# Output tiles whose two row halves swap PSUM banks midway, in a fused attention and feed-forward kernel

## The chip, the cores and the metric

The kernel runs on one core of a Trainium2 chip. The metric is the device time of one launch in microseconds (us), the median over several runs; for the kernel before it is 373.13 us (three runs, 372.79 to 373.79). A profiled execution of the same kernel gives the trace that is read below. The engines are called PE (TensorE matmul), PEld (TensorE weight load), DVE (VectorE), ACT (ScalarE), POOL (GpSimd) and SP (SyncE, which issues the stores).

## The reference

Attention with a softmax whose denominator has one term more, then a feed-forward layer with a squared ReLU. Cut to what matters:

```python
# q, k, v: (8, 12, 448, 64); w_in: (768, 2048); w_out: (2048, 768)
scores = scale * q @ k.T
e = exp(scores - max)
attn = e / (sum(e) + exp(-max) + 1e-9)
x = (attn @ v) laid out as (3584, 768)     # 8 * 448 tokens
r = maximum(x @ w_in, 0)
out = (r * r) @ w_out                      # (3584, 768), float32
```

Inputs come as float32 and are used as float16 on PE; sums are float32.

## The kernel before

**Work.** Batches are b = 0 to 7. Three heads' quads per batch (four heads each) go through scores, exponential, sums and values; the result, transposed, is x for the feed-forward layer. The hidden layer g = (max(x w_in, 0))^2 stands in a ring of two batches (`gs`), and the output is made from it in tiles of 128 tokens, each as two half tiles of 384 columns (`HALF`). A half tile is a sum over 16 blocks f of 128 hidden units.

**How a half tile is summed.** `out_piece` with `rows=True` (L553) cuts the 128 x 128 array in four parts of 64 x 64. For each f it issues four matmuls: two column parts (64 tokens each), and for each the array's upper rows (hidden units 0 to 63 of the block) into one PSUM bank (`op`), the lower rows (64 to 127) into another (`lo`). At the end each bank holds half of the sum, for all 128 tokens. `out_first` (L570) reads bank `op`, scales it and writes the SBUF tile `ot`, on DVE (L576) or on ACT (L574); `out_second` (L578) then reads `lo` on DVE (L580), adds `ot` and stores the half tile through the SP queue (`store`, L539). The order within a half tile is thus: 64 matmuls, first copy, add, store.

**The order is written by hand.** Strings of steps give the order of every instruction on all engines; each engine works its own steps strictly in that order, and semaphores are placed where a step needs another engine's result. The letters that matter here:

- `s` scores of a chunk on PE into one of two double banks (`sp`), `e` its exponential on ACT (L255), which frees the double bank; `v` the chunk's product with the values on PE (seven chunks, 0 to 6, per quad).
- `a` with step 0 to 3: the sum over the chunks on DVE (L439, L441, L443, L445); `S` the column sums on PE (needs `a` step 3, and takes a double bank), `Z` and `M` their logarithm and reciprocal on ACT (L461, L464), `X` the scaled values on DVE (L485).
- `o n,f0,f1`: `out_piece` of half tile n for blocks f0 to f1; `O n,act`: `out_first`, on ACT where act is 1; `Q n`: `out_second`.
- `J` and the letters A to I and U: the hidden layer, on full 128 x 128 matmuls (L663), with ACT and DVE work behind each.

**PSUM.** Eight banks: two double banks for `sp`, and a ring of four single banks (`mp`) which output tiles (two at a time), values (two at a time, `v` 0 until `X`) and the hidden layer share. A new tile takes the bank that was set free first in the written order, and its first matmul waits until the last reader of that bank is done.

**Three stretches hold the steps that the change touches.** The second list of steps (L880) works on batches 1 to 3 and the first 14 half tiles; its part from half tile 6 on ran at about 100 to 131 us. `CYCLE` (L935) is worked twice, for periods 4 and 6, with 14 half tiles each; in each the hidden layer comes first, then scores, exponentials, values and output tiles side by side (about 163 to 217 us and 249 to 304 us). What follows to the end of the kernel is not touched.

Of the kernel before, what the change touches and what calls it, by code (L numbers as in the profile page):

```python
# [17 lines left out]
def kernel(  # L18
# [235 lines left out]
    def exp(out_, in_):  # L254
        nc.scalar.activation(out=out_, in_=in_, func=AF.Exp, scale=scale)  # L255
# [174 lines left out]
    def quad_exp(m, c):  # L430
        exp(chunk_quad(m, c).rearrange("p (o x) -> p o x", o=2), sps.pop(("quad", m, c))[:, :, 0:S])

    def add_quad(m, step):

        a, z = eqs[m, 0], eqs.get((m, 1))
        w = 4 * S
        if step == 0:
            esq[m] = es_pool.tile([128, w], FP16, name="half")
            nc.vector.tensor_add(esq[m], a[:, 0:w], a[:, w:2 * w])  # L439
        elif step == 1:  # L440
            nc.vector.tensor_add(esq[m], esq[m], z[:, 0:w])  # L441
        elif step == 2:
            nc.vector.tensor_add(esq[m][:, 0:2 * S], esq[m][:, 0:2 * S], esq[m][:, 2 * S:w])  # L443
        else:
            nc.vector.tensor_add(esq[m][:, 0:2 * S], esq[m][:, 0:2 * S], z[:, w:w + 2 * S])  # L445
# [17 lines left out]
    def quad_reciprocal(m):  # L463
        nc.scalar.activation(out=zqs[m], in_=zqs[m], func=AF.Exp, scale=-1.0)  # L464
# [415 lines left out]
    for step in """  # L880
        S1 s44 v1,0 Z1 v1,1 v1,2 v1,3 v1,4 v1,5 s45 o0,0,2 v1,6 e44 o0,2,4 a2,0 o0,4,6 a2,1 M1 o0,6,8 s46 o0,8,10 X1 o0,10,12 e45 o0,12,14
        a2,2 a2,3 s47 o2,0,2 w0 e46 o2,2,4 e47 s48 o0,14,16 e48 o2,4,6 S2 O0,0 o2,6,8 o2,8,10 s49 o2,10,12 o2,12,14 Q0 Z2 s50 a3,0 v2,0
        o2,14,16 O2,0 Q2 e49 s51 v2,1 v2,2 v2,3 e50 e51 v2,4 w2 s52 v2,5 v2,6 a3,1 o1,0,2 o1,2,4 M2 o1,4,6 s53 o1,6,8 e52 o1,8,10 s54 e53
        o1,10,12 o1,12,14 s55 X2 e54 o1,14,16 o4,0,2 e55 a3,2 O1,0 s56 o4,2,4 o4,4,6 s57 o4,6,8 y1 o4,8,10 Q1 e56 a3,3 o4,10,12 e57 a4,0
        o4,12,14 s58 o4,14,16 v3,0 S3 v3,1 e58 O4,0 v3,2 v3,3 Z3 Q4 v3,4 a4,1 s59 v3,5 d26 d27 o3,0,2 s60 v3,6 a4,2 M3 o3,2,4 o3,4,6 e59
        o3,6,8 o3,8,10 X3 o3,10,12 s61 o3,12,14 e60 o3,14,16 o5,0,2 s62 o5,2,4 y2 w4 o5,4,6 e61 e62 a4,3 s63 o5,6,8 O3,0 y3 Q3 o5,8,10
        o5,10,12 o5,12,14 e63 a5,0 s64 o5,14,16 S4 O5,1 J0,1 A0 Q5 d24 d25 e64 y4 J1,1 J0,2 w1 J0,6 J1,2 C0 A1 J1,6 J0,5 U0 U1 B0 C1 w6 a5,1
        J1,5 J0,7 J1,7 D0 B1 G1 J1,3 J0,3 Z4 D1 J0,4 E0 J1,4 J2,1 F1 E1 J3,1 J3,2 F0 A2 J2,2 w3 H0 w5 C2 G0 J2,6 A3 U2 J3,6 J2,5 C3 J2,7 U3 M4
        J3,5 a5,2 w7 B2 B3 J3,7 D2 G3 D3 I0 G2 J2,3 J3,3 J2,4 F2 E3 J3,4 E2 s65 v4,0 s66 v4,1 F3 v4,2 H1 v4,3 e65 I1 H2 a5,3 H3 v4,4 v4,5 s67
        e66 o6,0,2 o6,2,4 v4,6 X4 I2 S5 e67 I3 o6,4,6 Z5 o6,6,8 s68 o6,8,10 e68 o6,10,12 s69 v5,0 e69 o6,12,14 o6,14,16 s70 O6,0 v5,1 e70 v5,2  # L890
        v5,3 M5 v5,4 v5,5 v5,6 Q6 a6,0 s71 e71 o7,0,2 o7,2,4 s72 X5 o7,4,6 e72 o7,6,8 o7,8,10 s73 o7,10,12 e73 o8,0,2 s74 o8,2,4 e74 o7,12,14
        a6,1 s75 e75 o7,14,16 a6,2 o8,4,6 s76 e76 o8,6,8 o8,8,10 a6,3 O7,0 s77 e77 o8,10,12 o8,12,14 S6 Q7 o8,14,16 v6,0 s78 v6,1 v6,2 v6,3
        v6,4 Z6 s79 O8,0 e78 v6,5 Q8 v6,6 e79 a7,0 o9,0,2 o9,2,4 M6 s80 o9,4,6 e80 o9,6,8 a7,1 s81 o9,8,10 o9,10,12 o9,12,14 o9,14,16 X6 s83
        e81 d28 o10,0,2 a7,2 s82 o10,2,4 o10,4,6 a7,3 e83 o10,6,8 s85 o10,8,10 O9,0 e82 o10,10,12 S7 Q9 o10,12,14 o10,14,16 v7,0 v7,1 e85 v7,2
        Z7 v7,3 s86 M7 O10,0 s84 v7,4 v7,5 Q10 o11,0,2 v7,6 e84 a8,0 o11,2,4 o11,4,6 o11,6,8 d31 o11,8,10 X7 o11,10,12 d29 o11,12,14 a8,1
        o11,14,16 o12,0,2 o12,2,4 o12,4,6 o12,6,8 O11,1 Q11 o12,8,10 e86 o12,10,12 o12,12,14 a8,2 o12,14,16 v8,0 a8,3 S8 v8,1 O12,1 v8,2 v8,3
        v8,4 v8,5 v8,6 Q12 o13,0,2 o13,2,4 d30 o13,4,6 o13,6,8 Z8 M8 o13,8,10 Y1 o13,10,12 o13,12,14 X8 o13,14,16 O13,1 Y2 Q13
    """.split():
        STEPS[step[0]](*(int(y) for y in step[1:].split(",")))

    def period(b):
# [38 lines left out]
        o0,0,2 F7 e0,0 I5 s0,1 e0,1 o0,2,4 H6 o0,4,6 o0,6,8 s0,2 o0,8,10 e0,2 o0,10,12 s0,3 H7 e0,3 I7 o0,12,14 I6 o0,14,16 s0,4 o1,0,2 e0,4  # L940
        o1,2,4 O0,0 Q0 s0,5 d1 o1,4,6 o1,6,8 s0,6 o1,8,10 e0,5 o1,10,12 s1,0 a0,0 o1,12,14 e0,6 o1,14,16 e1,0 a0,1 s1,1 a0,2 O1,0 e1,1 o2,0,2
        o2,2,4 s1,2 o2,4,6 o2,6,8 e1,2 s1,3 o2,8,10 o2,10,12 a0,3 e1,3 S0 Z0 o2,12,14 Q1 o2,14,16 s1,4 e1,4 v0,0 v0,1 v0,2 v0,3 M0 O2,0 v0,4
        Q2 v0,5 s1,5 o3,0,2 e1,5 s1,6 o3,2,4 a1,0 v0,6 o3,4,6 e1,6 o3,6,8 X0 s2,0 a1,1 o3,8,10 o3,10,12 e2,0 s2,1 a1,2 a1,3 o3,12,14 o4,0,2
        s2,2 e2,1 o4,2,4 o3,14,16 s2,3 o4,4,6 e2,2 O3,0 o4,6,8 e2,3 S1 Q3 o4,8,10 Z1 o4,10,12 o4,12,14 a2,0 v1,0 o4,14,16 s2,4 v1,1 M1 d3 v1,2
        O4,0 e2,4 Q4 v1,3 v1,4 s2,5 v1,5 v1,6 X1 o5,0,2 o5,2,4 e2,5 s2,6 o5,4,6 o5,6,8 a2,1 s3,0 a2,2 e2,6 o6,0,2 e3,0 o5,8,10 a2,3 s3,1 e3,1
        o5,10,12 o5,12,14 s3,2 e3,2 o6,2,4 o5,14,16 s3,3 e3,3 O5,0 o6,4,6 o6,6,8 Q5 S2 o6,8,10 o6,10,12 v2,0 a3,0 s3,4 o6,12,14 o6,14,16 Z2
        O6,0 s3,5 v2,1 v2,2 Q6 e3,4 s3,6 v2,3 v2,4 M2 v2,5 v2,6 X2 o7,0,2 o7,2,4 e3,5 e3,6 o7,4,6 s4,0 o7,6,8 o7,8,10 e4,0 s4,1 e4,1 o8,0,2
# [147 lines left out]
```

## Time and profile before

| | |
|---|---|
| median of three runs | 373.13 us (372.79 to 373.79) |
| profiled execution | 372.36 us, of which the span from first to last instruction is 370.3 us |
| granted TensorE clock | 1.00 |
| PE busy | 361.7 us (98% of the span) |
| ACT busy | 282.4 us (76%) |
| DVE busy | 275.7 us (74%) |

A page of the profile lists busy times, then 40 slices of the span, the DMA queues, the chain of work that ended last, groups of instructions by line, and DMA issues. In group rows, "x2688 | 133.2, 323" means 2688 instructions, 133.2 us in which at least one of them ran, and 323 ns as the mean length of one; after the next bar stands the idle time of the engine before them and what ended it. In a timeline row the first number is the start in us from the span's start, the second the length in us of that merged row; on PE, matmuls overlap, so a row reaches past the start of the next. What counts on PE is the distance from start to start. A row of a wait view reads: who waited, for whom, total us, how often, longest.

### The profile page before, as it was taken

The numbers are of one execution on the slowest core, as the hardware profiler recorded it, in microseconds if no ns is written. First come the engines' busy times: TensorE is split into PE (matmuls) and PEld (weight loads), VectorE is DVE, ScalarE is ACT, GpSimd is POOL, SyncE is SP. The second block draws the span as 40 slices with busy tenths as digits, with TensorE's granted clock in tenths as the row PEclk, the third lists the DMA queues.
The fourth block names the chain that finished last, engine by engine and source line by source line (L and its number), as shares of the span: only waits on it lengthen the run. The fifth ranks groups of instructions, "written<-read, shape, count | busy, mean of one in ns | idle before, by whom it ended". The sixth has DMA issues, their size and how long they took to land.

```text
span 370.3 us, 13666 instructions
## 1 busy us (share of the span) xinstructions
PE 361.7 (98%) x6024; PEld 248.8 (67%) x6024; DVE 275.7 (74%) x484; ACT 282.4 (76%) x413; POOL 62.3 (17%) x96
## 2 busy tenths in 40 slices
PE   8789999999999999999999999999999999999996
PEld 4566556669977755567799965557777765555664
DVE  3888898999987875867887874777878777885441
ACT  6899988987899645689999665679999748794221
POOL 8543350400400330400201060400200000000000
PEclk9999999999999999999999999999999999999999
DMA  8999999999777999905229669854212110001232
GB/s 138 203 205 205 204 198 206 226 225 189 154 146 133 190 181 191 134 2 114 62 58 156 154 118 180 162 64 99 61 53 66 47 62 5 2 0 44 86 85 88
DMA packets 75052, 45.31 MB, mean 122 GB/s; under 512 B 47473, under 2 KB 72945, under 8 KB 74993
## 3 DMA queue, kind: packets, MB, share of 16 engines
q0 software_dynamic: 24752, 22.62, 38.7%
q1 hardware_dynamic: 49952, 21.59, 27.0%
q8 instruction: 47, 0.77, 0.9%
q10 hardware_dynamic: 288, 0.23, 0.2%
q14 instruction: 13, 0.10, 0.1%
HBM read 45.69 MB, written 17.93 MB: 172 GB/s over the span
## 4 chain that ended last, share of the span: by engine, by line
PE 90%; ACT 4%; DVE 2%; DMA 2%; issue 1%; POOL 1%; POOLq 0%; DVEq 0%
PE mp L94 42%; PE mp L663 38%; PE sp L94 9%; ACT et L255 3%; DMA nn<-in_k_dram 2%; PE mp L208 1%; ACT rcp L373 1%; DVE qk L218 0%; ACT rcp L366 0%; DVE half L342 0%; DVE half L441 0%; DVE half L443 0%; DVE half L445 0%; DVE half L348 0%; DVE xt L485 0%
## 5 line engine op out<-in xcount | busy, mean ns | idle before, releaser
L255 ACT ACTIVATE et<-sp 128x896 f16<-128x896 f32 (+2 forms) x173 | 145.2, 899 | 7.6 <-PE sp L94 6.9
L94 PE MATMUL mp<-wout,gs 64*64 64x384 f16 (+1 forms) x2736 | 138.8, 322 | 0.2 <-issue 0.2
L94 PEld LDWEIGHTS <-gs 64*64 64x64 f16 (+1 forms) x2736 | 87.4, 107 | 21.7 <-issue 0.8
L663 PEld LDWEIGHTS <-win 128*128 128x128 f16 x480 | 46.4, 98 | 33.6 <-issue 1.2
L94 PE MATMUL sp<-qk 64*64 64x224 f16 (+1 forms) x1056 | 56.2, 273 | 2.3 <-issue 0.7
L663 PE MATMUL mp<-xt,win 128*128 128x448 f16 (+1 forms) x288 | 54.2, 329 | 0.0
L94 PEld LDWEIGHTS <-qk 64*64 64x64 f16 x1056 | 34.4, 114 | 14.5 <-issue 6.2
L189 POOL COPY flatq<-qk 64x384 f16<-64x384 f16 x20 | 15.3, 763 | 159.4 <-DMA qk<-stage_k 142.7
L94 PE MATMUL mp<-et,vn 64*64 64x448 f16 (+1 forms) x616 | 38.8, 345 | 0.0
L663 PE MATMUL mp<-et,win 128*128 128x448 f16 x144 | 32.8, 352 | 0.0
L576 DVE TENSOR_SCALAR ot<-mp 128x384 f32<-128x384 f32 x34 | 18.9, 556 | 18.0 <-PE mp L94 17.9
L663 PE MATMUL mp<-et,nn 128*128 128x448 f16 (+1 forms) x160 | 32.3, 350 | 0.0
L663 PEld LDWEIGHTS <-nn 128*128 128x128 f16 x216 | 21.0, 98 | 14.7
L666 ACT ACTIVATE qk<-mp 128x448 f32<-128x448 f32 (+1 forms) x33 | 16.8, 532 | 16.0 <-PE mp L663 15.9
L580 DVE SCALAR_TENSOR_TENSOR ot<-mp,ot 128x384 f32<-128x384 f32 x42 | 23.4, 556 | 6.7 <-ACT ot L574 4.0
L485 DVE TENSOR_TENSOR xt<-mp,rcp 128x448 f16<-128x448 f32 x42 | 24.2, 618 | 4.3 <-ACT rcp L464 2.2
L94 PEld LDWEIGHTS <-vn 64*64 64x64 f16 x756 | 22.7, 107 | 6.1 <-issue 0.5
L715 ACT ACTIVATE gs<-mp 128x448 f16<-128x448 f32 x28 | 14.2, 543 | 15.0 <-PE mp L663 13.3
L439 DVE TENSOR_TENSOR half<-et 128x1792 f16<-128x1792 f16 x21 | 23.0, 1097 | 1.2 <-ACT et L255 1.2
L660 DVE CUSTOM_DVE_ANT_0 gs<-mp,rcp 128x448 f16<-128x448 f32 x24 | 14.2, 619 | 13.0 <-ACT rcp L666 7.4
L441 DVE TENSOR_TENSOR half<-half,et 128x1792 f16<-128x1792 f16 x21 | 22.8, 1085 | 0.7 <-DVE half L439 0.5
L710 ACT ACTIVATE gs<-gs 128x448 f16<-128x448 f16 (+1 forms) x36 | 22.4, 657 | 1.1 <-DVE gs L660 1.1
(102 smaller groups left out, 450.2 us busy)
## 6 DMA issues: line engine op xcount, KB each, us to landing
out_dram<-ot SPq DMA_DIRECT2D x52, 96.0 KB, 3.5
out_dram<-ot SPq DMA_DIRECT2D x19, 192.0 KB, 2.0
win<-in_moe_w_in_dram POOLq DMA_DIRECT2D x8, 384.0 KB, 12.9
wout<-in_moe_w_out_dram POOLq DMA_DIRECT2D x4, 768.0 KB, 11.8
vn<-in_v_dram POOLq DMA_DIRECT2D x10, 288.0 KB, 5.6
stage_q<-in_q_dram POOLq DMA_DIRECT2D x4, 676.0 KB, 11.6
stage_k<-in_k_dram POOLq DMA_DIRECT2D x4, 676.0 KB, 14.4
nn<-in_q_dram POOLq DMA_DIRECT2D x8, 224.0 KB, 7.9
```

Source lines behind the costliest of these rows:

```text
L94: return nc.tensor.matmul(out_, lhsT, rhs, start=start, stop=stop)
L189: nc.gpsimd.tensor_copy(km[rows_].rearrange("p h (x o) -> p h x o", o=2)[:, :, :, odd], src[:, :, S // 2 - 32:S // 2])
L255: nc.scalar.activation(out=out_, in_=in_, func=AF.Exp, scale=scale)
L439: nc.vector.tensor_add(esq[m], a[:, 0:w], a[:, w:2 * w])
L441: nc.vector.tensor_add(esq[m], esq[m], z[:, 0:w])
L485: nc.vector.tensor_mul(xts[b][:, 2 * g + i, :], xqs[m][i][:, 0:S], zqs[m][:, i, :])
L576: nc.vector.tensor_scalar(out=ot, in0=op[:, 0:w], scalar1=OUT_SCALE, scalar2=None, op0=ALU.mult)
L580: nc.vector.scalar_tensor_tensor(out=ot, in0=lo[:, 0:w], scalar=OUT_SCALE, in1=ot, op0=ALU.mult, op1=ALU.add)
L660: nc.vector._custom_dve(TENSOR_ADD_SAT, out=out_, in0=ps, in1=t, s0=3.0e38, s1=0.0)
L663: nc.tensor.matmul(out_, lhsT=lhsT, rhs=rhs, start=begins and first, stop=last, skip_group_check=not begins)
L666: nc.scalar.activation(out=t[:, 0:w], in_=src[:, 0:w], func=AF.Copy, scale=scale_)
L710: nc.scalar.activation(out=out_, in_=out_, func=AF.Square)
```

## The change

For 16 of the 21 tiles that are summed by halves of the array's rows (tiles 3 to 6 in the second list, tiles 1 to 6 of each pass of `CYCLE`) the two half tiles of a tile are now summed together. A new step `h t,k` (`turn_piece`), k = 0 to 15, issues eight matmuls, as many as the two blocks of an `o` step that it replaces, at the same places of PE's order. In the first eight pieces (turn 0) the upper rows sum into the bank of half tile 0 and the lower rows into that of half tile 1; in the last eight (turn 1) they change places. So at the end each bank holds a complete sum.

Each bank is then read once: `K t` copies half tile 0 on ACT, `L t` half tile 1 on DVE, each followed by its store. The steps `O` and `Q` of these tiles are gone, and with them the add.

Upper and lower rows must not write one bank at the same time, so turn 1 has to begin after the last matmul of turn 0 is done. This is written as two waits: a step that is marked `*t` in the list waits for the last matmul of turn 0 of tile t, beside what it waited for before, and the first matmul of turn 1 waits for that step. The marked steps are, in the second list, `e70*3`, `e78*4`, `M7*5` (ACT) and `a8,3*6` (DVE); in `CYCLE` `e1,4*1`, `M1*2`, `e3,4*3` (ACT), `a4,0*4`, `a5,0*5` and `a5,3*6` (DVE). The other steps stand in the same order.

```diff
+    def turn_piece(tok, k):
+        if k == 0:
+            turns[tok] = (mp_tile(), mp_tile())
+        turn, k = divmod(k, NFFB // 2)
+        g = gs[:, :, tok % RING:tok % RING + 128]
+        for f in (2 * k, 2 * k + 1):
+            for y in (0, 64):
+                for r in range(2):
+                    x, n = 64 * r, r ^ turn
+                    ins = mm(turns[tok][n][y:y + 64, 0:HALF], g[x:x + 64, f, y:y + 64], wout[x:x + 64, f, HALF * n:HALF * n + HALF],
+                             start=(f == 0 and turn == 0), stop=(f == NFFB - 1 and turn == 1))
+                    if turn and f == 0 and (y, r) == (0, 0):
+                        behind(ins, turned[tok])
+        if turn == 0:
+            turned[tok] = ins
+
+    def behind(ins, other):
+        tc.add_manual_dep(ins.ins, other.ins.name, mybir.DependencyInfo(mybir.DependencyClass.Sync, mybir.DependencyReason.DATA),
+                          reason="sums of the other rows in the same bank")
+
+    def run(steps, text, first=0):
+        for step in text.split():
+            step, _, tile_ = step.partition("*")
+            ins = steps[step[0]](*(int(y) for y in step[1:].split(",")))
+            if tile_:
+                tok = 128 * (first + int(tile_))
+                behind(ins, turned[tok])
+                turned[tok] = ins
+
+    def turn_out(tok, n):
+        ot = osb_pool.tile([128, HALF], FP32, name="ot")
+        src = turns[tok][n][:, 0:HALF]
+        if n:
+            nc.vector.tensor_scalar(out=ot, in0=src, scalar1=OUT_SCALE, scalar2=None, op0=ALU.mult)
+        else:
+            nc.scalar.activation(out=ot, in_=src, func=AF.Copy, scale=OUT_SCALE)
+        store(tok, ot, HALF * n, HALF * n + HALF)
...
 # second list, from half tile 6 on
-        e66 o6,0,2 o6,2,4 v4,6 X4 I2 S5 e67 I3 o6,4,6 Z5 o6,6,8 s68 o6,8,10 e68 o6,10,12 s69 v5,0 e69 o6,12,14 o6,14,16 s70 O6,0 v5,1 e70 v5,2
+        s65 v4,0 s66 v4,1 F3 v4,2 H1 v4,3 e65 I1 H2 a5,3 H3 v4,4 v4,5 s67 e66 h3,0 h3,1 v4,6 X4 I2 S5 e67 I3 h3,2 Z5 h3,3 s68 h3,4 e68 h3,5 s69 v5,0
+        e69 h3,6 h3,7 s70 v5,1 e70*3 v5,2 v5,3 M5 v5,4 v5,5 v5,6 a6,0 s71 e71 h3,8 h3,9 s72 X5 h3,10 e72 h3,11 h3,12 s73 h3,13 e73 h4,0 s74 h4,1 e74
+        h3,14 a6,1 s75 e75 h3,15 a6,2 h4,2 s76 e76 h4,3 h4,4 a6,3 K3 s77 e77 h4,5 h4,6 S6 L3 h4,7 v6,0 s78 v6,1 v6,2 v6,3 v6,4 Z6 s79 e78*4 v6,5
+        v6,6 e79 a7,0 h4,8 h4,9 M6 s80 h4,10 e80 h4,11 a7,1 s81 h4,12 h4,13 h4,14 h4,15 X6 s83 e81 d28 h5,0 a7,2 s82 h5,1 h5,2 a7,3 e83 h5,3 s85
+        h5,4 K4 e82 h5,5 S7 L4 h5,6 h5,7 v7,0 v7,1 e85 v7,2 Z7 v7,3 s86 M7*5 s84 v7,4 v7,5 h5,8 v7,6 e84 a8,0 h5,9 h5,10 h5,11 d31 h5,12 X7 h5,13
...
-        a8,2 o12,14,16 v8,0 a8,3 S8 v8,1 O12,1 v8,2
+        a8,2 h6,7 v8,0 a8,3*6 S8 v8,1 v8,2
...
 # CYCLE
-        s2,2 e2,1 o4,2,4 o3,14,16 s2,3 o4,4,6 e2,2 O3,0 o4,6,8 e2,3 S1 Q3 o4,8,10 Z1 o4,10,12 o4,12,14 a2,0 v1,0 o4,14,16 s2,4 v1,1 M1
+        s2,2 e2,1 h2,1 h1,15 s2,3 h2,2 e2,2 K1 h2,3 e2,3 S1 L1 h2,4 Z1 h2,5 h2,6 a2,0 v1,0 h2,7 s2,4 v1,1 M1*2
...
-        s3,3 e3,3 O5,0 o6,4,6 o6,6,8 Q5 S2 o6,8,10 o6,10,12 v2,0 a3,0 s3,4 o6,12,14 o6,14,16 Z2 O6,0 s3,5 v2,1 v2,2 Q6 e3,4 s3,6
+        s3,3 e3,3 K2 h3,2 h3,3 L2 S2 h3,4 h3,5 v2,0 a3,0 s3,4 h3,6 h3,7 Z2 s3,5 v2,1 v2,2 e3,4*3 s3,6
...
-        a5,3 S5 O12,1 Q12 v5,1
+        a5,3*6 S5 v5,1
...
-    for b in range(FIRST_PERIOD, B, 2):
-        STEPS = period(b)
-        for step in CYCLE.split():
-            STEPS[step[0]](*(int(y) for y in step[1:].split(",")))
+    for b in range(FIRST_PERIOD, B, 2):
+        run(period(b), CYCLE, EARLY // 2 + KC * (b - FIRST_PERIOD) // 2)
```

The functions `exp`, `quad_exp`, `add_quad` and `quad_reciprocal` now return their instruction, so that the marked steps can be made to wait. The lists above are cut and their lines joined; the steps between are the same but for `o`, `O` and `Q` becoming `h`, `K` and `L`.

More of the change, by code (lines that the diff above doesn't have):

```diff
@@ L463, in quad_reciprocal @@
     def quad_reciprocal(m):
-        nc.scalar.activation(out=zqs[m], in_=zqs[m], func=AF.Exp, scale=-1.0)
+        return nc.scalar.activation(out=zqs[m], in_=zqs[m], func=AF.Exp, scale=-1.0)
     xqs = {}
@@ L901, in period @@
+    """)
     def period(b):
@@ L940 @@
[L940 to L947, printed above, removed]
@@ L955 @@
+        h6,2 a5,2 e5,6 h6,3 h6,4 L5 h6,5 h6,6 h6,7 v5,0 a5,3*6 S5 v5,1 v5,2 v5,3 v5,4 Z5 Y1 v5,5 v5,6 h6,8 M5 h6,9 h6,10 X5 h6,11 Y2 h6,12 h6,13
+        h6,14 h6,15 K6 L6 d13
     """
     for b in range(FIRST_PERIOD, B, 2):
-        STEPS = period(b)
-        for step in CYCLE.split():
-            STEPS[step[0]](*(int(y) for y in step[1:].split(",")))
+        run(period(b), CYCLE, EARLY // 2 + KC * (b - FIRST_PERIOD) // 2)
     TOK0 = (B - 2) * S
```

69 lines of the change are left out of this document (36 added, 33 removed).

## The prediction

> **What bounds the kernel now.** I read the page first, then the waits, then three stretches of the span, then the timeline of the places where the change puts a wait. The page names PE:
>
> ```profile
> PE 361.7 (98%) x6024; PEld 248.8 (67%) x6024; DVE 275.7 (74%) x484; ACT 282.4 (76%) x413; POOL 62.3 (17%) x96
> ...
> PE 90%; ACT 4%; DVE 2%; DMA 2%; issue 1%; POOL 1%; POOLq 0%; DVEq 0%
> ```
>
> A busy PE need not be a full one, so the distance from start to start decides. Timeline of PE:
>
> ```profile
> 201.57 1.19 PE L94 MATMUL mp<-wout,gs 64*64 64x384 f16 x24
> 202.55 0.41 PE L94 MATMUL sp<-qk 64*64 64x224 f16 x8
> 202.74 1.19 PE L94 MATMUL mp<-wout,gs 64*64 64x384 f16 x24
> ```
>
> 24 output matmuls take 202.55 - 201.57 = 0.98 us, 163 ns for four; 384 columns in 163 ns is one column in 0.42 ns, and the stretches, at a granted clock of 1.00, are filled like this almost without a hole (stretch, length, PE, PEld, DVE, ACT, ...):
>
> ```profile
> 96.00:131.00 35.00, 34.82 (x860) 26.90 (x861) 28.54 (x47) 28.98 (x37) 7.97 (x14) 1.00 0.78 145
> ...
> 164.00:217.00 53.00, 52.90 (x1408) 47.32 (x1404) 41.63 (x66) 46.86 (x56) 5.21 (x7) 1.00 0.52 104
> ...
> 249.00:304.00 55.00, 55.00 (x1432) 40.76 (x1431) 43.70 (x70) 48.32 (x59) 1.94 (x2) 1.00 0.23 63
> ```
>
> Here the reader sees two things: PE loses 0.18 + 0.10 + 0.00 us in the three stretches that change, and ACT is the next engine (46.86 of 53). The reads of the output banks wait for PE, and PE for none of them:
>
> ```profile
> DVE ot L576 <- PE mp L94: 17.9, 19, 1.8
> ...
> ACT ot L574 <- PE mp L94: 15.7, 10, 2.3
> ```
>
> **The change part by part.** The groups, by form, of the add and of the copy on DVE:
>
> ```profile
> L580 DVE SCALAR_TENSOR_TENSOR ot<-mp,ot 128x384 f32<-128x384 f32 x42 | 23.4, 556 | 6.7 <-ACT ot L574 4.0
> ...
> L576 DVE TENSOR_SCALAR ot<-mp 128x384 f32<-128x384 f32 x34 | 18.9, 556 | 18.0 <-PE mp L94 17.9
> ```
>
> *Matmuls.* 16 tiles x 128 before and after, same size, same places, same four parts in turn: nothing. What hides nothing also frees nothing: PE is at its rate already.
>
> *DVE.* 32 adds go (L580) and, of 32 first copies, the 25 that ran on DVE; 16 copies `L` come. 41 fewer x 0.556 = 22.8 us of DVE, none of it on PE's path but at one place, where `S1` (181 us) waits for `a1,3` that is queued behind such copies:
>
> ```profile
> 179.43 0.82 PE L94 MATMUL mp<-wout,gs 64*64 64x384 f16 x16
> 179.50 0.80 DVE L445 TENSOR_TENSOR half<-half,et 128x896 f16<-128x896 f16 x1
> ...
> 180.35 0.38 PE L94 MATMUL sp<-half,ones 64*64 64x448 f16 x4
> ```
>
> `S1` starts 0.05 us after L445 ends at 180.30. Before it PE issued 16 matmuls from 179.43, done issuing at 179.43 + 4 x 0.163 = 180.08: a hole of 0.27 us, which the lighter DVE should close. **-0.27.** The 0.05 also serves below as the way from DVE or ACT to PE.
>
> *Stores.* The same stores by count and size; both halves of a tile now come together. No row of PE or of a reader waits for SP's queue in these stretches, and SP's transposed loads behind the stores are for work 20 us later: nothing.
>
> *The wait on `a,3` of tile 6, three times.* In the old order the step that stands where `h6,7` will is the last of half tile 12, and ACT copies that half tile at once, so its start shows when those matmuls are done:
>
> ```profile
> 126.60 0.80 DVE L445 TENSOR_TENSOR half<-half,et 128x896 f16<-128x896 f16 x1
> ...
> 127.45 0.37 PE L94 MATMUL sp<-half,ones 64*64 64x448 f16 x4
> 127.48 0.49 ACT L574 ACTIVATE ot<-mp 128x384 f32<-128x384 f32 x1 [1.30 <-PE mp L94]
> ```
> ```profile
> 212.27 0.61 DVE L445 TENSOR_TENSOR half<-half,et 128x896 f16<-128x896 f16 x1
> ...
> 213.15 0.40 PE L94 MATMUL mp<-et,vn 64*64 64x448 f16 x4
> 213.34 0.40 PE L94 MATMUL sp<-half,ones 64*64 64x448 f16 x4
> 213.39 0.49 ACT L574 ACTIVATE ot<-mp 128x384 f32<-128x384 f32 x1 [2.33 <-PE mp L94]
> ...
> 213.79 1.01 ACT L461 ACTIVATE rcp<-sp,one_b 128x896 f32<-128x896 f32 x1
> ```
> ```profile
> 298.94 0.36 PE L94 MATMUL sp<-half,ones 64*64 64x448 f16 x4
> 298.96 0.49 ACT L574 ACTIVATE ot<-mp 128x384 f32<-128x384 f32 x1 [2.33 <-PE mp L94]
> ```
>
> `a5,3` ran at 212.27, long before `S5` needed it. Now it starts when the tile's matmuls are done, 213.39, takes 0.61 and 0.05 to PE: `S5` starts at 214.05 instead of 213.34, and everything on PE stands behind it, with only one `v` step (0.19) for cover. +0.71; likewise 127.48 + 0.61 + 0.05 - 127.45 = 0.69 (a step of 0.61; the 0.80 of that row is the odd one) and 298.96 + 0.66 - 298.94 = 0.68. **+2.1.** This is the firmest term.
>
> *The wait on `e3,4`, twice.* Where `h3,7` will end, DVE's copy of half tile 6 begins (190.56):
>
> ```profile
> 188.05 0.92 ACT L255 ACTIVATE et<-sp 128x896 f16<-128x896 f32 x1
> ...
> 189.27 0.42 PE L94 MATMUL mp<-et,vn 64*64 64x448 f16 x4
> ...
> 189.92 0.92 ACT L255 ACTIVATE et<-sp 128x896 f16<-128x896 f32 x1
> ...
> 190.56 0.56 DVE L576 TENSOR_SCALAR ot<-mp 128x384 f32<-128x384 f32 x1 [0.47 <-PE mp L94]
> ...
> 190.89 0.40 PE L94 MATMUL sp<-qk,flatq 64*64 64x224 f16 x8
> ```
>
> `e3,4` (189.92) moves to 190.56 and ends at 191.48; `s3,6` needs its double bank and started at 190.89, now 191.53: +0.64 a period. Queued behind `e3,4` on ACT are `M2` and `e3,5`, as late as PE itself by then, so nothing is added. In front, `K2` follows `e3,3`, at the earliest 188.05 + 0.80 = 188.85 (0.80 is the distance of two exponentials where ACT is full, 1.72 less 0.92 in a row further down), and is done 0.49 later; `v2,0` takes its bank, 189.34 + 0.05 against 189.27: +0.12. Together 0.76, **+1.5** for two periods.
>
> *The copies `K` on ACT.* 16 come, 7 old ones go. One costs ACT 213.79 - 213.39 = 0.40 where work is queued behind. That matters where PE waits for the next exponential. Timeline before, in the second list:
>
> ```profile
> 109.68 2.60 ACT L255 ACTIVATE et<-sp 128x896 f16<-128x896 f32 x3 [0.30 <-PE sp L94]
> ...
> 112.20 1.01 ACT L461 ACTIVATE rcp<-sp,one_b 128x896 f32<-128x896 f32 x1
> ...
> 112.49 0.36 PE L94 MATMUL sp<-qk 64*64 64x224 f16 x8
> ...
> 113.11 1.72 ACT L255 ACTIVATE et<-sp 128x896 f16<-128x896 f32 x2
> ...
> 114.01 0.82 PE L94 MATMUL mp<-wout,gs 64*64 64x384 f16 x16
> ```
> ```profile
> 120.97 0.95 ACT L464 ACTIVATE rcp<-rcp 128x896 f32<-128x896 f32 x1
> ...
> 121.88 0.49 PE L94 MATMUL mp<-wout,gs 64*64 64x384 f16 x8
> ```
>
> The last of the three `e` ended at 112.28; with `K3` ahead of it, about 0.35 later (0.40, less what ACT regains: the three are 0.84 apart and can be 0.80). `s78` started at 112.49, now at 112.63 + 0.05: +0.19. `e78` then starts some 0.3 later and ends at 114.32; turn 1 of tile 4 (the place of 114.01, by then 114.20) starts at 114.37: +0.17. For tile 5 `M7` would end at 121.92 even with no copy ahead; with `K4` some 0.25 later, at 122.22 with the way to PE, against 121.88: +0.3. **+0.65** in the second list. In each period `K3` stands before `e4,4`:
>
> ```profile
> 197.54 1.72 ACT L255 ACTIVATE et<-sp 128x896 f16<-128x896 f32 x2
> ...
> 198.75 0.41 PE L94 MATMUL sp<-qk,flatq 64*64 64x224 f16 x8
> ...
> 199.51 0.41 PE L94 MATMUL sp<-qk 64*64 64x224 f16 x8
> ```
>
> `e4,4` ends 0.92 after 197.54, 0.40 later with the copy, and 0.05 to PE makes 198.91 against 198.75 for `s4,6`: +0.15; `e4,5` ends at 199.26, so 199.71 against 199.51 for `s5,0`: 0.05 more. **+0.4** for both periods. `K1` and `K4` of the periods fall where ACT idles; `K5`, `K6` behind the last exponential.
>
> *The other waits* I cost at nothing: `e70` and `e1,4` start after the matmuls that they wait for and end just before turn 1 needs them (some 0.1 and 0.03 us to spare); `M1` starts 0.4 later, `e2,4` behind it has 0.6 to spare; `a4,0` starts 1.9 later, but `S4` has 0.5 to spare after DVE's lighter queue has caught up; `a5,0` starts earlier than now. If this cover is gone, each adds 0.1 to 0.6.
>
> *What no row shows*: a bank that the upper rows wrote and the lower rows add to. The Trainium skill, "TensorEngine Tiling (Array Packing)", section "Gotcha 1: PSUM Pressure", says that different row tiles cannot access one PSUM bank at the same time and that software has to synchronise them: that speaks against the change, since the old form with one bank for each row half never has to, and by that rule 16 turns pay a wait. No run here shows what happens without the wait. From rows, the bounds of a turn are 0 (the wait is over when PE arrives) and, if PE drained at each, the time from the last four matmuls' start, one slot of 0.16 ahead of the 213.15, to the copy that waits for them at 213.39: 0.40, and 16 x 0.40 = 6.4. I take 0, by the nearest rows: double banks change between PE and ACT at every `s` with no hole beyond the wait.
>
> *The sum*: -0.27 + 2.1 + 1.5 + 0.65 + 0.4 = **+4.4 us**. On the profiled execution 372.36 + 4.4 = 376.8; of those, 370.3 are span and 2.06 lie around it, which doesn't change. The median is 0.77 above that execution, so I put the median at 373.13 + 4.4 = **377.5**.
>
> **The rivals.**
>
> *Not slower: the reads of the banks were what mattered.* Fewer, shorter bank holds let PE run on, and the waits are over before PE comes. Against it: the three stretches hold 0.28 us of idle PE plus the hole of 0.27, so the most to win is 0.55, 372.6. It decides in favour of this only if `a5,3` were done before 213.29, 0.71 before it can be. The Trainium skill, "TensorEngine Tiling (Array Packing)", section "PSUM Bottleneck", says that after TensorE is sped up by tiling the copy out of PSUM may become the bottleneck; by that rule, 41 fewer reads should pay, and the wait rows above, where copies wait for PE, disagree.
>
> *No change.* PE has slack I don't see, or the wait lands elsewhere: 373.1. For it speaks only that all steps but the output's stand where they stood.
>
> *ACT becomes the bound.* If `K1` to `K4` of each period and `K3`, `K4` of the second list push every exponential behind them to PE, 10 x 0.40 = 4.0 takes the place of my 0.65 + 0.4 + 0.24 (the bank of `v2,0`): 4.4 + 2.7 = 7.1, 380.2. For it: ACT 46.86 of 53. Against: the 0.30 us of idle time in the row of 109.68, and the 6.1 us that ACT idles in that stretch of 53.
>
> *Every turn drains PE*: half of the bound, 16 x 0.20 = 3.2 more, 380.7. For it only that nothing here has such a turn; against it, the matmuls themselves stay in the same order of parts and banks.
>
> **How the numbers follow.** Chances: forecast 0.72, ACT as bound 0.10, drained turns 0.08, no change 0.07, not slower and gaining 0.03. 0.3% (1.1 us) is about what a measurement of this kernel can tell from no change; so slower 0.90, same 0.07, faster 0.03. The range leaves out half of the two high rivals and the low ones: from 375.2 (the firmest term alone, 373.13 + 2.1) to 380.0 (all terms and 2.5 us more: five of the covers above gone, or most of one high rival).
>
> **What would show it.** In the new profile: L445 of `a5,3` waiting for PE `mp`, and PE `sp` waiting about 0.7 us for L445, three times; PE `sp` waiting about 0.6 for L255 near 191 and 277 us; DVE busy about 253 us, ACT about 287; output matmuls still 163 ns for four. Wrong would be: no PE wait on L445; new gaps at the first matmul of each turn 1; or exponentials late by 0.4 after each `K` through to the stretch's end.

## The result, and the profile after

The changed kernel takes 377.88 us (median of 4 runs, 376.66 to 380.25), the kernel before in the same series 372.96 us (4 runs, 372.17 to 373.79). The ratio is 1.0132, with a 95% interval of 1.0106 to 1.0157: slower by 4.9 us. Forecast were 377.5 us and +4.4 us. In the series further down, one run each of own6, of noswap and of the kernel before came out far longer than the rest (474, 540 and 2139 us); they are in the medians, which they move by 0.04 us at most, and not in the ratios.

A run's time is its span from the first to the last instruction and something that lies around it. That is 2.06 to 2.17 us for the kernel before and 1.72 to 1.85 us for every other kernel here, the one with nothing but three waits added (before_wait) among them. So every comparison with the kernel before comes out some 0.3 us lower than the spans do: by spans the changed kernel is slower by 5.2 us (375.95 against 370.7, medians of `again` and of the kernel before beside it). Why less lies around the span is open.

The first profiled execution of the changed kernel took 380.25 us (span 378.4). Its row of the granted clock, one digit per 40th of the span, dips near the start, ahead of every stretch that the change touches, and the first 60 us took some 2.3 us longer there:

```profile
PEclk9879999999999999999999999999999999999999
```

So I read the main numbers from a second profile of the same kernel, taken in the run called `again` below: 377.15 us, span 375.4, granted clock 1.00 throughout. Its line of busy times, from the page:

```profile
PE 364.0 (97%) x6024; PEld 251.7 (67%) x6024; DVE 256.2 (68%) x443; ACT 284.2 (76%) x422; POOL 62.1 (17%) x96
```

DVE works 19.5 us less than before (275.7), with 41 instructions fewer, and the kernel is slower all the same: PE stays the engine that is full. The three stretches of the second list and the two passes of `CYCLE` (stretch, its length, then busy us and instructions of PE, PEld, DVE, ACT, POOL, the granted clock, the DMA share and GB/s):

```profile
95.00:131.00 36.00, 35.02 (x830) 26.85 (x832) 24.35 (x37) 29.67 (x40) 8.04 (x11) 1.00 0.81 137
163.00:217.00 54.00, 52.93 (x1355) 43.36 (x1357) 34.92 (x53) 47.89 (x62) 2.47 (x4) 1.00 0.48 96
249.00:304.00 55.00, 53.96 (x1353) 43.92 (x1351) 34.80 (x54) 49.46 (x65) 1.24 (x2) 1.00 0.23 58
```

PE is idle here for 0.98 + 1.07 + 1.04 = 3.1 us, where before it was idle for 0.28. Part of the loss does not show as idle time, because a matmul row reaches past the start of the next; the distances from start to start show all of it. Whom PE waited for (who, for whom, total us, how often, longest):

```profile
PE sp L94 <- DVE half L445: 1.8, 3, 0.6
PE sp L94 <- ACT et L255: 1.4, 3, 0.5
```

Both lines were forecast: `S8`, `S5`, `S5` wait for the marked `a,3` on DVE, and `s3,6` twice for the marked `e3,4` on ACT (0.45 us each; the third wait of that line, at 18.58 us, is in the kernel before as well). The first of the three on DVE, in the timeline:

```profile
128.11 0.36 PE L94 MATMUL mp<-et,vn 64*64 64x448 f16 x4
...
128.39 0.62 DVE L445 TENSOR_TENSOR half<-half,et 128x896 f16<-128x896 f16 x1 [1.17 <-PE mp L94]
...
129.06 0.38 PE L94 MATMUL sp<-half,ones 64*64 64x448 f16 x4 [0.60 <-DVE half L445]
```

A `v` step takes PE 0.19 us, so `S8` was due at 128.11 + 0.19 = 128.30 and started at 129.06. More closely resolved, the three gaps are 0.77, 0.81 and 0.81 us. The idle time that the last row names is 0.60: the rest is hidden in the tail of the matmul before, which is why a sum of waits comes out low. The wait on `e3,4`, first pass:

```profile
192.15 0.57 PE L94 MATMUL mp<-et,vn 64*64 64x448 f16 x8
192.21 0.92 ACT L255 ACTIVATE et<-sp 128x896 f16<-128x896 f32 x1 [0.44 <-PE mp L94]
...
193.17 0.39 PE L94 MATMUL sp<-qk,flatq 64*64 64x224 f16 x8 [0.45 <-ACT et L255]
```

After two `v` steps `s3,6` was due at 192.53 and came at 193.17, 0.04 after the exponential ended: 0.65 us, once in each pass.

**Does a turn itself cost PE anything?** Only where its wait is late. In 14 of the 16 turns the first matmul of turn 1 follows the matmuls before it with no gap (1 ns at most). In the two others the weight load names the late marker, `e78` for tile 4 and `M7` for tile 5:

```profile
113.86 0.59 PE L94 MATMUL mp<-et,vn 64*64 64x448 f16 x8
...
114.43 0.47 PEld L94 LDWEIGHTS <-gs 64*64 64x64 f16 x16 [0.40 <-ACT et L255]
...
121.99 0.57 PE L94 MATMUL mp<-et,vn 64*64 64x448 f16 x8
...
122.69 0.14 PEld L94 LDWEIGHTS <-gs 64*64 64x64 f16 x8 [0.56 <-ACT rcp L464]
```

These are gaps of 0.19 and 0.33 us. In the first profile, and in that of own6, a third turn was late, by about 0.3 us: tile 5 of the first pass, whose marked `a5,0` took 1.41 us there, beside a copy on POOL, and 1.09 in `again`. Nor do the output matmuls themselves get longer. Their group by form (count, busy us, mean ns, idle time before them and what ended it), first in the kernel before, then in the changed one:

```profile
L94 PE MATMUL mp<-wout,gs 64*64 64x384 f16 x2688 | 133.2, 323 | 0.2 <-issue 0.2
```
```profile
L94 PE MATMUL mp<-wout,gs 64*64 64x384 f16 x2688 | 133.5, 323 | 0.4 <-issue 0.2
```

### The profile page after: what moved, and what is told of

Same layout as the page of the kernel before. It is cut to its first block, busy times and chain, and to the rows that moved or that the text cites. A ratio compares the mean times of both kernels' runs of the same rounds, so it can differ in the third digit from the quotient of the medians.

```text
span 378.4 us, 13615 instructions
## 1 busy us (share of the span) xinstructions
PE 366.7 (97%) x6024; PEld 253.1 (67%) x6024; DVE 257.3 (68%) x443; ACT 284.4 (75%) x422; POOL 62.8 (17%) x96
## 4 chain that ended last, share of the span: by engine, by line
PE 88%; ACT 5%; DMA 2%; DVE 1%; issue 1%; POOL 1%; DVEq 0%; POOLq 0%; ACTq 0%
PE mp L94 41%; PE mp L704 37%; PE sp L94 9%; ACT et L255 3%; DMA nn<-in_k_dram 2%; PE mp L208 1%; DVE half L445 1%; POOL nn L118 1%; ACT rcp L373 1%; PE xp L94 0%; DVE half L439 0%; ACT rcp L366 0%; ACT rcp L464 0%; ACT rcp L461 0%; POOL vn L106 0%
## 5 line engine op out<-in xcount | busy, mean ns | idle before, releaser
L94 PE MATMUL mp<-et,vn 64*64 64x448 f16 (+1 forms) x616 | 39.8, 350 | 0.0
L439 DVE TENSOR_TENSOR half<-et 128x1792 f16<-128x1792 f16 x21 | 23.2, 1105 | 18.5 <-PE mp L94 10.5
L94 PEld LDWEIGHTS <-vn 64*64 64x64 f16 x756 | 24.7, 111 | 6.8 <-issue 1.9
L461 ACT ACTIVATE rcp<-sp,one_b 128x896 f32<-128x896 f32 x21 | 21.4, 1019 | 9.8 <-PE sp L94 9.8
L441 DVE TENSOR_TENSOR half<-half,et 128x1792 f16<-128x1792 f16 x21 | 23.0, 1093 | 2.3 <-ACT et L255 1.8
L753 DVE TENSOR_TENSOR gs<-gs 128x448 f16<-128x448 f16 (+1 forms) x48 | 22.2, 505 | 0.8 <-ACT gs L756 0.6
```

Of the source, the lines that this page charges most:

```text
L94: return nc.tensor.matmul(out_, lhsT, rhs, start=start, stop=stop)
L439: return nc.vector.tensor_add(esq[m], a[:, 0:w], a[:, w:2 * w])
L461: nc.scalar.activation(out=rcp, in_=zp[:, :, 0:S], func=AF.Ln, bias=one_b)
L753: nc.vector.tensor_mul(out_, out_, out_)
```

## The experiments

The times are medians in us. Runs in one block shared a chip and the runs of the kernel before.

| run | what it does | time | before | ratio (95%) |
|---|---|---|---|---|
| own6 | tile 6's wait on an instruction of its own | 375.38 | 373.13 | 1.0056 (1.0034 to 1.0077) |
| own63 | tile 3's wait in `CYCLE` too | 374.42 | 373.13 | 1.0040 (1.0019 to 1.0060) |
| noswap | no swap and no waits | 373.33 | 373.13 | 1.0009 (0.9986 to 1.0033) |
| before_wait | kernel before, with the three waits of tile 6 | 374.88 | 373.13 | 1.0045 (1.0025 to 1.0065) |
| again | the changed kernel | 377.76 | 372.86 | 1.0126 (1.0104 to 1.0148) |
| k_dve4 | copies `K` of tiles 1 to 4 on DVE | 376.49 | 372.86 | 1.0100 (1.0070 to 1.0129) |
| pool_held | POOL copies held until `S8`, `S5` | 377.29 | 372.86 | 1.0125 (1.0094 to 1.0157) |
| all_own | 13 of 16 waits on instructions of their own, `K` as in k_dve4 | 372.32 | 372.86 | 0.9980 (0.9966 to 0.9994) |
| pool_beside | POOL copies made to start with the marked step | 377.39 | 373.09 | 1.0119 (1.0092 to 1.0145) |
| all_own2 | all_own again | 372.02 | 373.09 | 0.9975 (0.9954 to 0.9996) |

### own6: tile 6's wait on an instruction of its own

```diff
+    mark_ = consts.tile([128, 1], FP32)
+    def mark(tok):
+        ins = nc.vector.tensor_copy(mark_, one_b)
+        behind(ins, turned[tok])
+        turned[tok] = ins
...
+        "N": lambda t: mark(128 * t),
-        a8,3*6 S8
+        a8,3 N6 S8
-        a5,3*6 S5
+        a5,3 N6 S5
```

> The changed kernel with the wait of tile 6 taken off the fourth step of the sum (a8,3 and a5,3) and given to a one-column DVE copy of its own, put right behind that step; the other turns as they were. Theory (PE stands where a marked step that PE soon needs is held back): the three waits of PE for L445, 2.5 us in the view of waits and 1.15 + 1.11 + 0.81 = 3.1 us by starts, go away, and about 3.0 us with them: 374.9, some 1.9 above before. Rival 1 (a turn costs by itself, whoever carries the wait): the gap moves to the first matmul of turn 1 of tile 6, 377 to 378. Rival 2 (the copies on ACT are the cost): 377 to 378, gaps spread over the scores.

Measured: 375.38 us, 2.25 above before, where the changed kernel is 4.9 above. More was expected, since the 3.1 us of gaps were those of the first profile, two of which a copy on POOL had made longer; in `again` the three are 2.39. The timeline of own6 at the place of the first such wait:

```profile
127.21 0.63 DVE L445 TENSOR_TENSOR half<-half,et 128x896 f16<-128x896 f16 x1
...
128.42 0.36 PE L94 MATMUL sp<-half,ones 64*64 64x448 f16 x4
...
128.45 0.15 DVE L639 COPY mark__106<-one_b 128x1 f32<-128x1 f32 x1 [0.62 <-PE mp L94]
```

`a8,3` runs early again, `S8` no longer waits, and the tiny copy carries the wait at 128.45. PE's waits no longer hold a line for L445. The same dependence between the same matmuls is still there; only the instruction that carries it is another. So the 2.65 us between the two kernels (2.39 us by the gaps) is not the price of the turn, but of having hung it on a step that PE needs at once.

### own63: tile 3's wait in `CYCLE` too

```diff
-        e3,4*3 s3,6
+        e3,4 N3 s3,6
```

> As own6, and the wait of tile 3 in both periods taken off the exponential e3,4 and given to a one-column DVE copy as well. Theory: the 0.65 us that PE waits for its double bank at s3,6 goes away twice, 1.3 us more than own6: 373.6. Rival 1 and rival 2: as own6, no gain.

Measured: 374.42 us, another 0.96 us less (the 373.6 expected started from too low a time for own6). The timeline of own63:

```profile
193.41 0.95 ACT L255 ACTIVATE et<-sp 128x896 f16<-128x896 f32 x1
...
193.98 0.15 DVE L639 COPY mark__106<-one_b 128x1 f32<-128x1 f32 x1 [0.58 <-PE mp L94]
...
194.40 0.39 PE L94 MATMUL sp<-qk,flatq 64*64 64x224 f16 x8
```

The exponential starts before the matmuls of turn 0 are done (the copy at 193.98 shows when they are), and `s3,6` shows no wait longer than the pipeline hides. Start to start 0.10 us is left of 0.65, so 2 x 0.54 = 1.1 us should go, and 0.96 did. The 0.10 that is left is there without any wait too (noswap).

### noswap: the new order and the single reads, without the swap

```diff
-                    x, n = 64 * r, r ^ turn
+                    x, n = 64 * r, r
-                    if turn and f == 0 and (y, r) == (0, 0):
-                        behind(ins, turned[tok])
...
-                behind(ins, turned[tok])
```

> The changed kernel with the swap left out: upper rows sum into the bank of half tile 0 and lower rows into that of half tile 1 in both turns, so each half tile sums over half of the hidden units only; all waits for the turns are gone, matmuls, copies and stores are the same in number and place. Theory: only the delays by the copies on ACT stay (0.19 at s78, 0.1 at v2,0 and at s4,6 in each period) less the hole at S1: 373.1 to 373.7. Rival 1: the same, 373. Rival 2 (the copies are the cost): 376 to 378.

Measured: 373.33 us, 0.2 above before (0.5 by spans, 371.5 against 371.0), with an interval that holds 1 and ends at 1.2 us more. So most of the loss sits in the waits; the reads, copies and stores in their new form cost some 0.5 us, 1.5 at the most. What the copies `K` cost on ACT is still there, in the timeline of noswap:

```profile
113.13 0.36 PE L94 MATMUL mp<-et,vn 64*64 64x448 f16 x4
...
113.50 0.40 PE L94 MATMUL sp<-qk 64*64 64x224 f16 x8
```

`s78` comes 0.37 after a `v` step of 0.19: the 0.19 us forecast for it.

### before_wait: the three waits alone, in the kernel before

```diff
-            nc.vector.tensor_add(esq[m][:, 0:2 * S], esq[m][:, 0:2 * S], z[:, w:w + 2 * S])
+            last = nc.vector.tensor_add(esq[m][:, 0:2 * S], esq[m][:, 0:2 * S], z[:, w:w + 2 * S])
+            if m in (8, 14, 20):
+                tc.add_manual_dep(last.ins, newest[0].ins.name, ...)     # newest: last matmul of half tile 12
```

> The kernel before with one thing alone added: a8,3 and, in both periods, a5,3 also wait for the last matmul of half tile 12, as they wait for tile 6 in the changed kernel. Theory: 0.7 us on PE each time, 2.1 in all, and up to 0.35 more where POOL copies run beside the step, as they did twice in the changed kernel: 375.1 to 375.8. Rival 1 (the turn): no turn here, 373.0. Rival 2: 373.0.

Measured: 374.88 us, a ratio of 1.0045, so 0.9 to 2.4 us more, and a little less than expected. The three gaps in its profile are 0.79, 0.83 and 0.80, 2.42 in all, at the upper edge of that; by spans the difference is 2.1 us (373.1 against 371.0). These waits alone are thus enough to make the kernel before slower, without any swap. This run also has both readers of the same matmuls side by side, the ACT copy that served as the yardstick of the prediction and the step that waits:

```profile
127.84 0.36 PE L94 MATMUL mp<-et,vn 64*64 64x448 f16 x4
...
128.05 0.49 ACT L577 ACTIVATE ot<-mp 128x384 f32<-128x384 f32 x1 [1.30 <-PE mp L94]
128.14 0.62 DVE L445 TENSOR_TENSOR half<-half,et 128x896 f16<-128x896 f16 x1 [0.99 <-PE mp L94]
...
128.82 0.38 PE L94 MATMUL sp<-half,ones 64*64 64x448 f16 x4 [0.62 <-DVE half L445]
```

The DVE step starts 0.09 us after the ACT copy, though both wait for the same matmul. That is what the forecast of this term missed.

### again: the changed kernel once more

> The changed kernel once more, so that the three below have it from the same chip: 377 to 378; PE waits 0.8 to 1.1 us for L445 three times and 0.65 for L255 twice.

Measured: 377.76 us against 372.86, the same 4.9 us. Its profile is the one read above.

### k_dve4: the copies `K` of tiles 1 to 4 on DVE

```diff
-    def turn_out(tok, n):
+    def turn_out(tok, n, late=False):
-        if n:
+        if n or late:
...
-        "K": lambda t: turn_out(128 * t, 0),
+        "K": lambda t: turn_out(128 * t, 0, t < 5),
```

> The changed kernel with the copies K of tiles 1 to 4 on DVE in place of ACT, waits as they are. Theory: what the copies on ACT delay goes (0.19 at s78, 0.19 and some of 0.33 at turn 1 of tiles 4 and 5, 0.1 at v2,0 and at s4,6 in each period), the waits at S8, S5 and s3,6 stay: 0.8 to 1.1 us under the changed kernel, 376.6 to 377.0. Rival 2 (the copies on ACT are most of the cost): 373 to 374.

Measured: 376.49 us, 1.27 less than `again`. In its profile the gaps at `s78`, at `v2,0` and at `s4,6` are gone, 0.06 is left of tile 4's 0.19 and 0.10 of tile 5's 0.33, together 0.19 + 0.21 + 0.21 + 0.13 + 0.23 = 1.0 us; the gaps of `S8`, `S5` and `s3,6` stay (0.81, 0.79, 0.79 and 0.62 twice). (That execution took 379.14 us, the longest of the six; in it alone PE waits 1.6 us for a load of keys near 102 us.) So these ten copies on ACT cost about 1.0 to 1.3 us, not the 4.0 us that ACT as the bound would have made.

### pool_held and pool_beside: a copy on POOL beside the marked step

In the first profile of the changed kernel, two of the three marked steps on DVE were longer than in `again`, each with a copy of keys on POOL that began just ahead of it. Timeline:

```profile
130.70 1.51 POOL L189 COPY flatq<-qk 64x384 f16<-64x384 f16 x2 [2.07 <-DMA qk<-stage_k]
130.73 1.00 DVE L445 TENSOR_TENSOR half<-half,et 128x896 f16<-128x896 f16 x1 [1.57 <-PE mp L94]
...
218.72 1.51 POOL L189 COPY flatq<-qk 64x384 f16<-64x384 f16 x2 [6.57 <-DMA qk<-stage_k]
218.79 0.96 DVE L445 TENSOR_TENSOR half<-half,et 128x896 f16<-128x896 f16 x1 [2.11 <-PE mp L94]
```

There the gaps at `S8` and `S5` were 1.15 and 1.11 us. The two runs try to keep the copies away from the step, and to bring them to it:

```diff
 # pool_held: first copy of the pair waits for the last matmul of S
+                if hold and r == 0:
+                    behind(c, newest[0])
-        a8,3*6 S8
+        a8,3*6 S8 d32
-        a5,0*5 d11 ... a5,3*6 S5
+        a5,0*5 ... a5,3*6 S5 d11
```

> The changed kernel with the POOL copies that ran beside the marked step of tile 6 (second list and period 4) held back until S8 and S5 are issued. If POOL's copies make that DVE step longer (1.00 and 0.96 us beside them, 0.63 in period 6 where there are none), the step takes 0.63 in all three and PE's gaps at S8 and S5 fall from 1.15 and 1.11 to about 0.8: 0.6 to 0.7 us less than the changed kernel. If the length has another cause, nothing changes.

```diff
 # pool_beside: it waits for the last matmul of turn 0 of tile 6
-        h6,7 v8,0
+        h6,7 d32 v8,0
-        a5,0*5 d11 ... h6,7 v5,0
+        a5,0*5 ... h6,7 d11 v5,0
```

> The changed kernel with the second pair of POOL copies (second list and period 4) held until the last matmul of turn 0 of tile 6, the same event that the marked DVE step waits for. If a POOL copy that starts first makes the DVE step wait, that step takes about 1.0 us in these two places and 0.63 in period 6 (no copies), PE's gaps at S8 and S5 are 1.1, 1.1 and 0.8, and the time is 0.6 to 0.7 above the changed kernel, 378.4. If whichever starts first goes on unhindered and DVE starts first, 0.63 and 0.8 in all three and POOL's copy is the longer one. If they don't meet, nothing changes.

Measured: 377.29 and 377.39 us, against 377.76 for `again`, with ratios (1.0125, 1.0119, 1.0126) that can't be told apart. Neither could show it. In `again` no marked step was lengthened, so holding the copies had nothing to remove; and in pool_beside the copy still came after the DVE step (129.02 against 128.68), because its keys landed late, and the step took 0.62. What POOL does to DVE here is read from the rows of all twelve profiles, in the last section; no run forces it.

### all_own and all_own2: nearly every wait on an instruction of its own

To own63 and k_dve4 this adds the other waits: of the 16, only those on `e70` and the two `M1` stay where they were.

```diff
-        e78*4 ... M7*5 ... e1,4*1 ... a4,0*4 ... a5,0*5
+        e78 N4 ... M7 N5 ... e1,4 N1 ... N4 a4,0 ... N5 a5,0
```

> The swap kept, its waits carried in 13 of 16 turns by one-column DVE copies of their own (all but e70 and the two M1), copies K of tiles 1 to 4 on DVE. Theory: no gap is left that the change brought, and the hole at S1 (0.27) may close: 372.8 to 373.3, the same as before. Rival 1 (a turn costs by itself, up to 0.4 each): 376 to 379.

> The kernel of all_own once more, to tell 0.998 from 1: theory (all gaps that the change brought are gone, nothing is won on PE but the hole of 0.27 at S1): 0.998 to 1.000 of before.

Measured: 372.32 us against 372.86 (0.9980, 0.9966 to 0.9994) and 372.02 against 373.09 (0.9975, 0.9954 to 0.9996). Both intervals lie just below 1, and the difference is below the 0.3% that I had called the limit. Of the 0.5 and 1.1 us, 0.3 lie outside the span, where every kernel but the one before is shorter; by spans it is 0.15 us (370.55 against 370.7) and 0.7 (370.25 against 370.95). So this form is level with the kernel before or better by a few tenths of a microsecond, and beats the changed one by some 5 us. The stretches of all_own2:

```profile
95.00:131.00 36.00, 35.75 (x875) 27.23 (x872) 26.06 (x45) 29.20 (x38) 8.37 (x13) 1.00 0.83 139
163.00:217.00 54.00, 54.00 (x1427) 41.21 (x1427) 37.01 (x61) 47.23 (x58) 5.32 (x9) 1.00 0.49 99
249.00:304.00 55.00, 55.00 (x1429) 41.59 (x1418) 37.39 (x62) 47.73 (x58) 1.24 (x2) 1.00 0.21 60
```

In the two passes PE is not idle at all, and all 16 turns begin without a gap. The wait for tile 6 in its timeline:

```profile
127.16 0.36 PE L94 MATMUL sp<-half,ones 64*64 64x448 f16 x4
...
127.19 0.15 DVE L639 COPY mark__106<-one_b 128x1 f32<-128x1 f32 x1 [0.38 <-PE mp L94]
```

## Why the prediction was right, by its steps

The time came 0.4 us above the forecast, inside the range. The mechanism of its large terms is shown by the runs; that the total came so close is in part luck, since smaller errors cancel. The terms, as gaps on PE from start to start in `again`:

| term of the sum | forecast, us | measured, us |
|---|---|---|
| the wait on `a,3` of tile 6, three times | +2.1 | +2.39 |
| the wait on `e3,4` and the bank of `v2,0`, twice | +1.5 | +1.50 |
| `s78`, turns of tiles 4 and 5, second list | +0.65 | +0.70 |
| `s4,6` and `s5,0`, twice | +0.4 | +0.21 |
| the hole ahead of `S1` | -0.27 | -0.08 |
| sum | +4.4 | +4.7 (median: +4.9) |

Measured from the first scores of a stretch to the first matmul of the hidden layer behind it (98.58 to 131.50 us before, for the first), the three stretches take 1.63, 1.60 and 1.74 us longer than before, 4.97 in all, of which the gaps of the table are 4.7. Another 0.13 is lost at a wait in the hidden layer between them, and 0.31 is saved around the span: 4.8 us, which is the difference of the two profiled executions, 377.15 - 372.36. The prediction had it that what lies around the span "doesn't change"; the work itself was forecast 0.7 us too low, and the smaller rest hid nearly half of that.

**The wait on `a,3`.** Place, direction and mechanism were right, and own6 and before_wait show them by taking the wait away and by adding it alone. The size was 0.1 short each time. I read the end of the matmuls from an ACT copy that waits for them, which starts 0.36 us after the last matmul's start in the rows before; the DVE step starts 0.42 to 0.43 after it in `again`, and before_wait has the difference in one view (128.05 and 128.14). The engine is not what makes it: DVE's one-column copies in own6 wait for the same matmuls and start 0.37 us after the last one's start, much as those copies on ACT do (0.36 to 0.37). But ahead of the marked step the trace has an instruction of DVE's sequencer that waits for PE in its place (EVENT_SEMAPHORE; the first in `again` ends at 128.34), and the step starts 0.04 us after that one ends. Ahead of the copies no such instruction waits for PE; they carry that wait themselves. So the yardstick was an instruction that waits in another way.

**The wait on `e3,4`.** Right to 0.02 us a period, with a yardstick on another engine than the one that waits: the copy on DVE at 190.56 started 0.36 us after the last matmul's start, and `e3,4` on ACT starts 0.37 after it in `again`. Both carry their wait for PE themselves.

**The copies `K`.** Together 0.91 us by gaps, without `v2,0`, where I had 1.05: `s4,6` lost 0.11 for 0.15, and `s5,0` nothing. k_dve4 shows that these gaps come from `K`.

**The hole ahead of `S1`: the step that failed.** I had it that `a1,3` "is queued behind such copies" and that the lighter DVE would close the hole. In `again` 0.20 us of it are left (0.10 in the first profile), since the copies were not what made `a1,3` late. The kernel before shows it by itself: in its second pass the queue holds the same copies, and there is no hole. `a1,3` is done in time, and `S1` follows 0.65 us, four times 0.163, after the matmuls ahead of it began:

```profile
265.17 0.62 DVE L445 TENSOR_TENSOR half<-half,et 128x896 f16<-128x896 f16 x1
265.34 0.82 PE L94 MATMUL mp<-wout,gs 64*64 64x384 f16 x16
...
265.99 0.36 PE L94 MATMUL sp<-half,ones 64*64 64x448 f16 x4
```

What differs is when POOL's copies run: from 177.40 to 179.88 us in the first pass, beside these steps, and from 260.61 to 262.60 in the second, over when `a1,1` begins at 263.32. The DVE and POOL rows of the kernel before, ahead of `S1` of the first pass:

```profile
177.40 2.48 POOL L189 COPY flatq<-qk 64x384 f16<-64x384 f16 x2 [24.73 <-DMA qk<-stage_k]
...
177.41 1.08 DVE L441 TENSOR_TENSOR half<-half,et 128x1792 f16<-128x1792 f16 x1
178.53 0.87 DVE L443 TENSOR_TENSOR half<-half 128x896 f16<-128x896 f16 x1
```

of `again`:

```profile
178.29 1.29 POOL L189 COPY flatq<-qk 64x384 f16<-64x384 f16 x2 [23.98 <-DMA qk<-stage_k]
...
179.04 1.42 DVE L441 TENSOR_TENSOR half<-half,et 128x1792 f16<-128x1792 f16 x1
180.50 0.62 DVE L443 TENSOR_TENSOR half<-half 128x896 f16<-128x896 f16 x1
...
181.06 0.82 PE L94 MATMUL mp<-wout,gs 64*64 64x384 f16 x16
181.23 0.62 DVE L445 TENSOR_TENSOR half<-half,et 128x896 f16<-128x896 f16 x1
...
181.91 0.38 PE L94 MATMUL sp<-half,ones 64*64 64x448 f16 x4
```

and of all_own2:

```profile
175.12 0.62 POOL L189 COPY flatq<-qk 64x384 f16<-64x384 f16 x1
...
177.10 1.08 DVE L441 TENSOR_TENSOR half<-half,et 128x1792 f16<-128x1792 f16 x1
178.22 0.62 DVE L443 TENSOR_TENSOR half<-half 128x896 f16<-128x896 f16 x1
...
178.94 0.62 DVE L445 TENSOR_TENSOR half<-half,et 128x896 f16<-128x896 f16 x1
179.12 0.82 PE L94 MATMUL mp<-wout,gs 64*64 64x384 f16 x16
...
179.77 0.36 PE L94 MATMUL sp<-half,ones 64*64 64x448 f16 x4
```

In all three, PE is done with the matmuls ahead of `S1` 2.67 us after `a1,1` (L441) begins: 180.08 - 177.41, 181.06 + 0.65 - 179.04, 179.12 + 0.65 - 177.10. The chain `a1,1`, `a1,2`, `a1,3` begins at the same distance with the heavy queue and with the light one, so the queue is not its cause. In all_own2, with POOL's copy long over, it takes 178.94 + 0.62 + 0.05 - 177.10 = 2.51 us, and there is no hole. In the kernel before, beside POOL's copies, two of its steps are longer by 0.25 and 0.18; 0.43 less the slack of 0.16 is the hole of 0.27. In `again` `a1,1` is longer by 0.34, and the hole is 0.20. The other profiles fit as well. In the first pass, nine of the twelve have copies of POOL beside these steps, which are longer by 0.25 to 0.55 us in all, and each has a hole of that less 0.15 (0.10 to 0.40 us); the three without (own6, k_dve4, all_own2) have none. In the second pass no copy runs beside them in any profile, and eleven of the twelve have no hole (in own63 one of 0.21, where the whole chain began 0.36 us later). No run moved that copy on purpose, but nothing in the rows speaks for the heavy queue.

**Costed at nothing.** The other waits, the stores and the matmuls' new order showed no gap, as forecast. DVE's busy time fell to 256 us, not to 253, though the adds and copies that went sum to 22.9 us in the groups, as forecast. The page counts time in which two instructions of an engine overlap once; the lengths of all of DVE's instructions sum to 300.1 us before and 278.5 in `again`, 21.6 less, so the overlap is most of the difference. ACT rose to 284, not to 287.

**The rivals.** *Every turn drains PE*: refuted by 14 turns of 16 in `again` and 16 of 16 in all_own2 that begin without a gap. The row drawn on was the right one: a wait that is over when PE arrives costs PE nothing. The rule of the Trainium skill ("TensorEngine Tiling (Array Packing)", section "Gotcha 1: PSUM Pressure"), that software must keep row tiles from one bank at the same time, was kept in every run that swaps. What it cost to keep it was some 3.5 us (the three waits of tile 6 and the two of tile 3, taken away in own63) or nothing that shows as a gap (all_own2), by where the wait was put. *ACT becomes the bound*: refuted, k_dve4 moves just the ten copies that this rival priced at 4.0 us, and wins 1.0 to 1.3. *No change*: refuted for this kernel, though noswap shows that it would nearly hold without the waits. *Not slower, since the reads mattered*: refuted for the kernel as changed; in all_own and all_own2, with the waits off the path, 0.15 and 0.7 us are won by spans. What there was to win is thus about as small as the 0.55 us of holes that I gave as the most; in all_own2 the hole ahead of `S1` (0.27) is closed, in all_own 0.2 of it is left.

## What to carry to other kernels

A wait between two engines costs what is queued behind the instruction that carries it, so hang it on an instruction that nobody soon needs: here a one-column copy of 0.15 us did for nothing what a needed step did for 0.65 to 0.8 us. Before counting on less work for an engine, look whether anybody waits for that engine: all_own2, with DVE busy for 14.9 us less than before (260.8 against 275.7), is 0.7 us faster by spans, and all_own 0.15, since PE was the bound. And when a wait is priced by the start of another instruction that waits for the same thing, see whether both carry the wait themselves: here an instruction that waited in the step's place went with 0.06 to 0.09 us of difference, and the engine with none.
